# Linear attention with a SoLU feed-forward: 24 early steps change engine, and the later steps get a new order

## The chip, the cores and the metric

The kernel runs on one core of a Trainium2 chip. The metric is device time in microseconds for one execution. The core has one queue of instructions for each engine: TensorE (PE; its weight loads are shown apart, as PEld), VectorE (DVE), ScalarE (ACT), GpSimd (POOL), and SyncE (SP), which here only issues DMAs.

## The reference

```python
def _attn_ref(q, k, v):                     # each [8, 8, 576, 64]
    q_s = np.exp(q - np.max(q, axis=-1, keepdims=True))
    q_s = q_s / (np.sum(q_s, axis=-1, keepdims=True) + 1e-09)
    k_s = np.exp(k - np.max(k, axis=2, keepdims=True))
    k_s = k_s / (np.sum(k_s, axis=2, keepdims=True) + 1e-09)
    kv = np.einsum('bhsd,bhse->bhde', k_s, v)
    return np.einsum('bhsd,bhde->bhse', q_s, kv)
...
def _moe_ref(x, w_in, w_out, g_ln):         # x [4608, 512]
    h = x @ w_in                            # [4608, 1024]
    e = np.exp(h - np.max(h, axis=-1, keepdims=True))
    solu = h * (e / (np.sum(e, axis=-1, keepdims=True) + 1e-09))
    mu = np.mean(solu, axis=-1, keepdims=True)
    var = np.mean((solu - mu) ** 2, axis=-1, keepdims=True)
    return ((solu - mu) / np.sqrt(var + 1e-06) * g_ln) @ w_out
```

The attention's output, with the heads side by side, is x.

## The kernel before

**The work.** There are eight batches, and 36 tiles of 128 rows. For each batch the keys (steps `K0` to `K7`) and the queries (`Q0a`, `Q0b`, `Q0c`, ..., and `R` for the rests) get their softmax, the keys are multiplied with the values, and attention (`x`) gives the transposed rows of x. For each tile or pair of tiles the hidden product (`h` for one tile, `H` for a pair by seven half products instead of eight) is followed by the row work: softmax, normalization, division into a high and a low f16 part (`h`, or `U` for a pair), and the product with `w_out` (`o`, or `O` and `E` for a pair). `w`, `y`, `W`, `Z` scale and split the weights, `T` and `TO` make the sums and differences of weight blocks that the pairs need; `LQ`, `LK`, `V` are loads, `P` is warm-up work for TensorE.

**Who sets the order.** The work is written as Python generators. A string, `ORDER`, is read from left to right; each word names a generator, which goes on to its next `yield`, and this is one step. `*n` repeats the word. The string has 1819 steps. The instructions of all engines are issued in that order, so each engine's queue has its own part of it, and an instruction at the head of a queue waits for its operands while all behind it on that engine wait too.

**Who does a step.** Where the code says `on(default)`, the operation is done by the default engine, or by VectorE when the word ends in `.v`. The default of the element operations between two tensors, and of the small per-row scalars, is GpSimd; the default of casts and copies is ScalarE. The names that the diff touches are: `am`, `pi`, `p`, `ph` (lines 829 to 838: scalars of one column that the pass at line 842 needs), `z`, `var`, `r`, `rr` (scalars of the normalization), `u` (lines 172 and 174 for the high part, 852 for the low part), `split` (the same for x), `qT`, `vm` and `swap` (copies), `iw` (line 326, a difference of weight blocks), and `ob` and `ott` of `TO` (lines 1009, 1013, 1019).

**Buffers.** A second table, `SLOTS`, says for each tile in the order of its making which buffer it takes: 25 pages of SBUF, four PSUM banks, and two PSUM places `h` of 128x1024 for hidden rows. A tile that takes a used buffer waits until the former one has been read.

**The place that the prediction comes to most.** `H27` is one of the pairs in the later part. Its first steps in the code are:

```python
t2 = ps.tile([P, DF], F32, name=f"h{name_of(row_tiles[1])}", **place("h", 2))
product(t2[:, left], "11", "11")
yield
t1 = ps.tile([P, DF], F32, name=f"h{name}", **place("h", 2))
product(t1[:, left], "12", "21")
yield
cast(on(nc.scalar), w_, t2[:, left])
yield
product(t2[:, left], "s2", "t2", True)
```

So a pair's second product of the left half waits for a copy (`vw<-h`) of the first, and both wait until the two places `h` are free.

Of the kernel before, what the change touches and what calls it, by code (L numbers as in the profile page):

```python
# [17 lines left out]
P = 128  # L18
# [17 lines left out]
    ),  # L36
    "bank": (
# [3 lines left out]
    ),  # L41
    "h": (
        "0 1 0 1 0 1 0 1 0 1 0 1 0 1 0 0 1 1 0 1 1 0 0 1 1 0 0 1 1 0 0 1 1 0 0 1 "
    ),
}
ORDER = (
# [53 lines left out]
)  # L100


@with_exitstack
def linear_attention_solu_ffn(ctx: ExitStack, tc: tile.TileContext, q, k, v, w_in, w_out, g_ln, out):

# [1139 lines left out]
```

## Time and profile before

| what | value |
|---|---|
| median of three runs | 442.11 us (441.96 to 442.28) |
| the profiled execution's own time | 440.85 us |
| span of its instructions | 439.1 us |
| instructions | 9202 |
| busy share PE, DVE, ACT, POOL | 95%, 88%, 74%, 72% |
| mean granted clock of TensorE | 0.997 |

The span runs from the first to the last instruction that the profiler recorded; 1.75 us of the execution's time lie around it. The profiled execution is 1.26 us shorter than the median of the three runs, so sums are made against 440.85 us and their difference is then set against 442.11 us.

### The profile page before, as it was taken

The numbers are of one execution on the slowest core, as the hardware profiler recorded it, in microseconds if no ns is written. First come the engines' busy times: TensorE is split into PE (matmuls) and PEld (weight loads), VectorE is DVE, ScalarE is ACT, GpSimd is POOL, SyncE is SP. The second block draws the span as 40 slices with busy tenths as digits, with TensorE's granted clock in tenths as the row PEclk, the third lists the DMA queues.
The fourth block names the chain that finished last, engine by engine and source line by source line (L and its number), as shares of the span: only waits on it lengthen the run. The fifth ranks groups of instructions, "written<-read, shape, count | busy, mean of one in ns | idle before, by whom it ended". The sixth has DMA issues, their size and how long they took to land.

```text
span 439.1 us, 9202 instructions
## 1 busy us (share of the span) xinstructions
PE 417.4 (95%) x3441; PEld 218.1 (50%) x3441; DVE 385.5 (88%) x765; ACT 323.4 (74%) x555; POOL 316.1 (72%) x336
## 2 busy tenths in 40 slices
PE   2798899999999999999999999999999999999995
PEld 1444344454454444544544445445444445666885
DVE  5999999999898998889988869999999998988952
ACT  3799998696796689878875677768685686785920
POOL 4206983889998879859966888886939897778340
PEclk9999999999999999999999999999999999999998
DMA  8989788489799696499996568994533665379982
GB/s 277 409 306 315 154 152 233 91 206 245 173 223 184 150 192 135 90 224 217 186 251 146 126 147 188 247 215 95 78 72 82 111 144 104 63 172 188 231 204 73
DMA packets 182620, 77.93 MB, mean 177 GB/s; under 512 B 162088, under 2 KB 171312, under 8 KB 182576
## 3 DMA queue, kind: packets, MB, share of 16 engines
q1 hardware_dynamic: 182576, 77.35, 77.0%
q8 instruction: 27, 0.44, 0.4%
q14 instruction: 17, 0.14, 0.1%
HBM read 36.70 MB, written 9.44 MB: 105 GB/s over the span
## 4 chain that ended last, share of the span: by engine, by line
PE 73%; POOL 8%; ACT 8%; DVE 6%; issue 3%; DMA 1%; ACTq 0%; POOLq 0%; DVEq 0%
PE o L1113 24%; PE h L734 18%; PE h L811 12%; PE kv L471 3%; PE x L666 3%; PE o_2y L1049 2%; PE o_0y L1049 2%; PE o_0x L1049 1%; PE o_2z L1049 1%; PE o_0z L1049 1%; PE o_2x L1049 1%; POOL qm L523 1%; POOL r L882 1%; POOL qhl L548 1%; POOL am L829 1%
## 5 line engine op out<-in xcount | busy, mean ns | idle before, releaser
L1113 PE MATMUL o<-wo,uT 128*128 128x512 f16 x624 | 141.4, 379 | 0.0
L1113 PEld LDWEIGHTS <-uT 128*128 128x128 f16 x624 | 60.3, 98 | 72.7 <-issue 1.6
L811 PE MATMUL h<-wi,xT 128*128 128x512 f16 x240 | 54.4, 379 | 0.0
L734 PE MATMUL h<-wt,split 128*128 128x512 f16 x198 | 46.2, 379 | 0.9 <-ACT vw L172 0.9
L734 PEld LDWEIGHTS <-split 128*128 128x128 f16 x264 | 25.5, 98 | 31.7 <-issue 2.5
L457 POOL TENSOR_TENSOR km<-km,kb 128x1152 f32<-128x1152 f32 x12 | 33.6, 2808 | 4.9 <-ACT kb L435 3.2
L811 PEld LDWEIGHTS <-xT 128*128 128x128 f16 x240 | 23.1, 98 | 27.5 <-issue 0.6
L548 POOL TENSOR_TENSOR qhl<-qm,qhl 128x512 f16<-128x512 f32 x24 | 28.8, 1220 | 3.0 <-ACT qhl L172 2.9
L734 PE MATMUL h<-wi,xT 128*128 128x512 f16 x132 | 30.8, 379 | 0.1
L734 PEld LDWEIGHTS <-xT 128*128 128x128 f16 x198 | 19.1, 98 | 23.6 <-issue 1.8
L803 PE MATMUL h<-iw,xT 128*128 128x512 f32 x64 | 29.5, 602 | 1.2 <-ACT e L866 1.2
L541 POOL TENSOR_TENSOR qm<-qm,qrec 128x1024 f32<-128x1024 f32 x13 | 25.6, 1966 | 6.3 <-DVE qrec L532 6.0
L523 POOL TENSOR_TENSOR qm<-qm,qnmx 128x1024 f32<-128x1024 f32 (+1 forms) x14 | 25.3, 1810 | 5.7 <-DVE qnmx L521 5.5
L825 ACT ACTIVATE e<-h,nm,hs 128x1024 f32<-128x1024 f32 x20 | 24.0, 1202 | 0.5
L852 POOL TENSOR_TENSOR u<-e,u 128x1024 f16<-128x1024 f32 x8 | 17.6, 2200 | 9.0 <-ACT u L172 4.6
L1126 ACT ACTIVATE os<-o,rr 128x512 f32<-128x512 f32 x23 | 15.7, 684 | 11.0 <-PE o L1113 7.9
L521 DVE TENSOR_REDUCE qnmx<-qm 128x16 f32<-128x1024 f32 (+1 forms) x17 | 19.2, 1147 | 4.3 <-DMA qm<-in_q_dram 4.3
L829 POOL TENSOR_SCALAR am<-top 128x1 f32<-128x1 f32 x21 | 10.9, 518 | 15.2 <-DVE top L819 14.2
L525 ACT ACTIVATE qm<-qm 128x1024 f32<-128x1024 f32 (+1 forms) x17 | 17.1, 1003 | 5.9 <-POOL qm L523 5.9
L471 PE MATMUL kv<-vm,km 64*64 64x65 f32 x1152 | 19.3, 219 | 2.0 <-ACT km L459 0.9
L459 ACT ACTIVATE km<-km 128x1152 f32<-128x1152 f32 x16 | 18.5, 1163 | 3.4 <-POOL km L457 3.2
L471 PEld LDWEIGHTS kv<-vm,km 64*64 64x64 f32 x1152 | 18.0, 134 | 5.8 <-issue 3.3
(330 smaller groups left out, 1057.6 us busy)
## 6 DMA issues: line engine op xcount, KB each, us to landing
out_dram<-os SPq DMA_DIRECT2D x32, 256.0 KB, 3.0
km<-in_k_dram SPq DMA_DIRECT2D x7, 1152.0 KB, 7.3
vm<-in_v_dram SPq DMA_DIRECT2D x28, 288.0 KB, 4.3
qm<-in_q_dram SPq DMA_DIRECT2D x7, 1024.0 KB, 6.7
wo<-in_moe_w_in_dram SPq DMA_DIRECT2D x4, 512.0 KB, 8.8
w_in<-in_moe_w_in_dram SPq DMA_DIRECT2D x4, 512.0 KB, 9.2
wo<-in_moe_w_out_dram SPq DMA_DIRECT2D x4, 512.0 KB, 4.4
w_out<-in_moe_w_out_dram SPq DMA_DIRECT2D x4, 512.0 KB, 6.8
```

The source lines that it names most:

```text
L457: on(nc.gpsimd).tensor_tensor(km[:, ns], km[:, ns], wide, op=ALU.subtract)
L471: nc.tensor.matmul(o, km[half, n, c], vm[half, n, c], start=(m == 0 and c == 0), stop=(m == 1 and c == KC - 1))
L521: nc.vector.tensor_reduce(shaped(nmx), x, axis=AX.X, op=ALU.max, negate=True)
L523: on(nc.gpsimd).tensor_tensor(x, x, wide(nmx), op=ALU.add)
L541: on(nc.gpsimd).tensor_tensor(x, x, wide(rec), op=ALU.mult)
L548: on(nc.gpsimd).tensor_tensor(lo, y, hi, op=ALU.subtract)
L734: nc.tensor.matmul(out, lefts[left](s, i), right_block(right, r, i), start=(n == 0 and not onto), stop=(n + 1 == len(terms)), skip_group_c ...
L803: nc.tensor.matmul(h[:, ns], xT[:, kc], iw[kc][:, ns], start=(i == 0), stop=(i == NP - 1))
L811: nc.tensor.matmul(h[:, ns], xT[:, t, kc], wi[:, s, kc, ns], start=(i == 0), stop=(i == len(terms) - 1))
L825: nc.scalar.activation(e, h, AF.Exp, bias=nm, scale=hs, accum_out=z)
L1049: nc.tensor.matmul(accs[acc], t[:, j, first + f], out_block(right, s, f), start=(f == n == 0 and not onto), stop=(f + 1 == NF // 2 and n = ...
L1113: nc.tensor.matmul(o, uT[:, j, f], wo[:, s, f, cols], start=(f == 0 and j == 0 and s == 0), stop=(f == NF - 1 and j == 1))
```

## The change

The same 1819 steps are done. The first 1168 of them (up to the step `H22#1`, the second step of pair 22, some 273 us into the span) keep their order, and 24 of them change engine. The 651 later steps come in a new order, and 113 of them change engine too. `SLOTS` differs only where the later steps make their tiles. The 24 early ones are (the number of the step in its generator counts from 0):

| step | operation | before | after |
|---|---|---|---|
| Q0b#6 | copy of qT | ACT | DVE |
| V03#1 | copy of vm | DVE | ACT |
| h1#7, h16#5, h19#3 | pi, ph, pi | POOL | DVE |
| h0#15, h4#18, h12#17 | z | POOL | DVE |
| o1#0, o8#0 | rr | POOL | DVE |
| h6#8, h8#8, h11#8, h12#8, h11#19 | am, am, am, am, var | POOL | DVE |
| T#1 | iw, 128x512 | POOL | DVE |
| K4#5 | four copies of swap | ACT | DVE |
| x13#10, h19#8 | f16 cast of split, of u | ACT | DVE |
| h15#3 | pi | POOL | DVE |
| h15#5, o15#0, h20#2, h20#3 | ph, rr, am, pi | DVE | POOL |

Among the later ones, `TO#0` to `TO#3` (the four `ob<-wo` sums of 128x1024, line 1009) go from DVE to POOL. `Q6a#6`, `K7#9`, `Q7a#1` and `x29#11` (each an element operation between two tensors) go from POOL to DVE, as do the low parts of u of tiles 22 and 25. The low part of u of tile 21 goes from DVE to POOL.

```diff
--- before.py
+++ after.py
...
     "h": (
-        "0 1 0 1 0 1 0 1 0 1 0 1 0 1 0 0 1 1 0 1 1 0 0 1 1 0 0 1 1 0 0 1 1 0 0 1 "
+        "0 1 0 1 0 1 0 1 0 1 0 1 0 1 0 0 1 1 0 1 1 0 0 1 0 1 1 0 0 1 1 0 0 1 1 0 "
     ),
...
-    "K0*3 w2 K0 P Q0b V03.v Q0a Q0c.v Q0c Q0a K0.v K0 K0.v K0*2 Q0c Q0c.v w3 w2 K0*2 w3*2 Q0a x0 K0 w0*2 x0 w1*2 "
+    "K0*3 w2 K0 P Q0b.v V03 Q0a Q0c.v Q0c Q0a K0.v K0 K0.v K0*2 Q0c Q0c.v w3 w2 K0*2 w3*2 Q0a x0 K0 w0*2 x0 w1*2 "
...
-    "Q6c o15 o16 h20 S5.v Q6a o16 h21 V70 o16*2 h21.v Q6c h21 H22*2 V71 S5 TO.v K6*3 h17 Q6c.v*2 h20 Q6c Q6a V72 "
-    "H22*2 K6*2 H22*3 h21 o17.v o17 K6 H22.v H22 h21 h20*2 Q6a*2 S5 Q6a K7 H22 K6 H22*3 h19 H22*2 h20*4 K7 LQ7*2 "
-    "o17 x24 h21.v TO.v h23*4 h21*2 h22*6 K6*3 S6 K7*4 h19 TO.v K7 Q6a o19*2 TO.v o19 Q7a h21 h21.v o19*3 K7 o17*4 "
...
-    "o22 h23 K7*2 o22*2 h25*3 S7 o22 h24 h25 Q7a TO h24 h24.v Q7a.v h24 R7 K7*2 o19 TO.v*2 H27*4 h24 S7 Q7c H27*3 "
-    "x29 o21*2 h24.v o23 H27.v H27*2 h24*2 x29*2 h25 h25.v h25*2 x29*2 H27 Q7a x29.v H27*3 o21*2 TO h25 o22 o24.v "
...
+    "h20 h21 o16 h20*3 LK7 h21*2 Q6a o16 h20 Q6a Q6c o15 o16 h20 S5.v Q6a o16 h21 V70 o16*2 h21.v Q6c h21 H22*2 TO "
+    "K6 h21 K6*2 h17 h19 V72 Q6a H22.v V71 H22*2 h21 Q6c h19 K7*5 Q6a o17*3 H22*2 Q6a Q6a.v Q6c.v K6 h20*4 H22 Q6a "
...
+    "h22 h23*3 h23.v h23*2 o19 S5 o19*2 o20*2 x24.v o17 K7 K7.v K7 TO h22*2 TO R5 S6.v Q7c x27*4 o20 h22 x27 H24 "
+    "Q7a Q7a.v h23 H24 LQ7 H24 TO x27*3 TO o20*2 H24*3 h21*2 h21.v H24 TO Q6c x29*3 H24.v h21.v LQ7 H24 x27 R7 H24 "
...
+    "h25*2 o22.v o22 H27 h23 H27.v x29*2 Q7a S5 h24.v h24 H27*3 h25 h25.v o22*2 h24 h24.v H27*3 Q7a*3 K7*3 Q7c "
+    "h25*3 S7 R7 o22 h25 h24 R7*2 H27*2 x29.v TO Q7a h25 H27*2 o21 H27*2 U27.v R7.v U27 o22.v h24 o24.v o24 U27*2 "
...
```

## Rows read from the trace of the kernel before

**Rows 1.** The page: its head, and the busy time of each engine.

```profile
span 439.1 us, 9202 instructions
...
PE 417.4 (95%) x3441; PEld 218.1 (50%) x3441; DVE 385.5 (88%) x765; ACT 323.4 (74%) x555; POOL 316.1 (72%) x336
```

**Rows 2.** Busy time by windows; columns: window, length, each engine, clock, DMA share, GB/s.

```profile
0.00:21.60 21.60, 10.59 (x169) 6.10 (x169) 15.83 (x36) 11.52 (x16) 7.72 (x12) 1.00 0.94 342
21.60:62.40 40.80, 37.00 (x298) 17.89 (x299) 39.46 (x70) 39.34 (x67) 24.34 (x22) 1.00 0.89 241
62.40:173.40 111.00, 110.35 (x866) 52.07 (x866) 102.00 (x181) 87.03 (x160) 90.60 (x111) 1.00 0.82 181
173.40:275.50 102.10, 101.87 (x944) 49.46 (x944) 88.67 (x203) 77.37 (x135) 81.60 (x89) 1.00 0.80 178
...
295.00:318.80 23.80, 23.80 (x268) 11.87 (x267) 21.59 (x50) 17.82 (x31) 19.68 (x20) 1.00 0.46 85
318.80:342.00 23.20, 21.77 (x101) 9.61 (x99) 22.25 (x42) 16.45 (x26) 13.55 (x12) 1.00 0.41 88
...
434.60:439.10 4.50, 0.00 (x0) 0.00 (x0) 0.48 (x1) 0.00 (x0) 0.00 (x0) 0.71 0.51 117
```

**Rows 3.** What TensorE waited for over the whole span: total, times, longest.

```profile
PE h L734 <- ACT vw L172: 1.1, 2, 0.9
...
PE h L734 <- DVE top L770: 0.5, 1, 0.5
PE wide_out L191 <- DVE p_kv L201: 0.4, 1, 0.4
```

**Rows 4.** The chain that ended last, 280 to 335 us: start, length, what.

```profile
311.77 3.29 POOL ob L1013
...
318.85 1.30 DVE e L842 x2
...
322.26 0.49 ACT vw L172
...
330.52 0.61 DVE h L770
```

**Rows 5.** Groups of equal instructions, engine by engine: busy time, mean ns of one.

```profile
L1013 POOL TENSOR_TENSOR ob<-ob,ob 128x1024 f32<-128x1024 f32 x2 | 5.7, 2844 | 0.0
L829 POOL TENSOR_SCALAR am<-top 128x1 f32<-128x1 f32 x21 | 10.9, 518 | 15.2 <-DVE top L819 14.2 <-DVE part L411 0.8
...
L852 DVE TENSOR_TENSOR u<-e,u 128x1024 f16<-128x1024 f32 x4 | 4.9, 1233 | 0.0
L1009 DVE TENSOR_TENSOR ob<-wo 128x1024 f32<-128x1024 f16 x4 | 4.9, 1221 | 0.0
...
L172 ACT COPY qT<-qt 128x512 f32<-128x512 f32 x4 | 2.3, 576 | 0.0
L172 ACT COPY vm<-wi 128x576 f32<-128x576 f32 x3 | 1.9, 672 | 2.5 <-DMA wi<-in_v_dram 2.5
```

**Rows 6.** The timeline of DVE and of POOL, 47 to 63 us.

```profile
50.81 1.22 DVE L284 TENSOR_SCALAR gw<-gw 128x1024 int32<-128x1024 int32 x1
53.09 0.68 DVE L284 TENSOR_SCALAR gw<-gw 128x1024 int32<-128x1024 int32 x1
57.16 1.21 DVE L286 SCALAR_TENSOR_TENSOR gw<-w_out,gw 128x1024 int32<-128x1024 int32 x1
...
48.71 0.79 POOL L870 TENSOR_SCALAR z<-z,p 128x1 f32<-128x1 f32 x1
49.58 1.90 POOL L541 TENSOR_TENSOR qm<-qm,qrec 128x1024 f32<-128x1024 f32 x1
...
56.20 2.26 POOL L829 TENSOR_SCALAR am<-top 128x1 f32<-128x1 f32 x1
```

**Rows 7.** The timeline of ACT and of DVE, 166 to 179 us.

```profile
167.76 1.04 ACT L172 CAST split<-sums 128x1024 f16<-128x1024 f32 x1
...
171.24 1.34 DVE L335 SCALAR_TENSOR_TENSOR wt<-iw,s_in,wt 128x1024 f16<-128x1024 f32 x1 [1.61 <-ACT wt L333]
```

100 rows, old and new, of tables (ORDER, SLOTS) are left out of this document.

## Prediction

> **What bounds the kernel.** I began with the page's head and the busy shares [rows 1]: TensorE is busy for 417.4 of 439.1 us. The question is therefore where the other 21.7 us are, and whether the change can reach them. VectorE with 88% is the next to be full.
>
> The windows answer the first half [rows 2]. TensorE is idle for 21.60 - 10.59 = 11.01 us in the first window, for 40.80 - 37.00 = 3.80 in the second, for 111.00 - 110.35 = 0.65 in the third and 102.10 - 101.87 = 0.23 in the fourth. From 318.8 to 342.0 it is idle for 23.20 - 21.77 = 1.43, and in the last window for all 4.50 (the last pass and the store). That makes 21.62, so all the rest holds 0.1 us. The granted clock is 1.00 in every window with matmuls in it; TensorE's own work costs the same in both orders, as no matmul is added or taken away. What can be won by a new order behind 273 us is thus about those 1.43 us, since the last 4.50 us come after the last matmul and their steps keep their form.
>
> Then I looked for what ended these waits. The list of TensorE's waits [rows 3] names a copy on ScalarE (`vw`, longest 0.9) and a VectorE pass (line 770, 0.5). The chain [rows 4] shows how they came to be: GpSimd makes an `ob` difference that takes 3.29 us at 311.77, only then come its one-column scalars, and VectorE's two passes over `e` wait for these until 318.85. The read of the hidden rows by the first of those frees the place that pair 27 needs; its `vw` copy ends at 322.75 and TensorE goes on. The second wait ends when VectorE's line 770 has run at 330.52. In 318.8 to 342.0 VectorE is busy for 22.25 of 23.20 us [rows 2], so it comes late to everything there. In the window before it GpSimd was busy for 19.68 of 23.80 us.
>
> **The 24 early steps.** TensorE loses 0.65 + 0.23 us between 62.4 and 275.5 us [rows 2], so an edit there can win at most this, and loses only if a step comes late by more than its lead.
>
> First, the two copies in the first 20 us. `qT` leaves ScalarE and `vm` comes to it: 0.672 - 0.576 = 0.10 us more at worst [rows 5], ahead of the exponentials that the keys wait for. If the old place of the copy was off the path it is nothing. I take 0.04.
>
> Second, 47 to 63 us, where VectorE has hardly a gap (39.46 of 40.80 us busy in the window [rows 2]) and where the weights' scales are late: TensorE waits 0.4 us for `wide_out` [rows 3]. `pi` and `z` come to VectorE there. The trace has no row for these two on VectorE at this place. From below, an `am` or `z` that delays nothing costs nothing; from above, one takes no longer than the 0.518 us mean of the `am` group on GpSimd [rows 5], so 2 x 0.52 = 1.04. On the other side, GpSimd's `z` of 0.79 us at 48.71 is gone, and its pass over `qm` (1.90 us at 49.58) ends earlier. A VectorE pass that began under that pass took 1.22 us, and its like at 53.09 took 0.68 [rows 6]: up to 0.54 us may come back. I take +0.10, between -0.5 and +0.5, because the passes of VectorE follow each other without a gap while the end of the chain also hangs on other engines' sums.
>
> This is one place for the Trainium skill. The row shows a VectorE pass of 1.22 us beside a GpSimd pass and 0.68 us alone [rows 6], and a one-column `am` on GpSimd at 56.20 that took 2.26 us and ended at 58.46, just behind VectorE's two-tensor pass that ended at 58.37. The Trainium skill, "SBUF — State Buffer", "Who interferes with whom", says that the two engines share a pair of SBUF ports as an exclusive lock, which a VectorE instruction with two SBUF inputs also takes against a GpSimd instruction that reads SBUF, and that the loser is blocked until the other ends. The trace agrees at these two places; by that rule alone, moving work between these two engines frees nothing, and the gain of the later part would be 0 and the sum 442.11 + 0.08 = 442.2.
>
> Third, the cast of `split` at 167.76, 1.04 us, leaves ScalarE; its later work there comes earlier, and VectorE's idle 1.61 us before 171.24 [rows 7] holds the cast's time on VectorE (below: nothing; above: the 1.23 us of the nearest pass of this shape [rows 5]). Two short waits of TensorE at 173 and 179 us are for such copies and make up the 0.23 us of that window [rows 2]. I take -0.06, between -0.23 and 0.
>
> The other early edits are one-column scalars, a 128x512 difference, four swap copies and one cast of `u`. I cost them at nothing: they are hidden by TensorE's work, which between 62.4 and 275.5 us stands still for only 0.88 us, though VectorE has 111.00 - 102.00 = 9.0 and 102.10 - 88.67 = 13.4 us of idle time [rows 2] to take them. Without this cover the sum of their VectorE time, below 4 us, would be the price.
>
> **The later part.** I priced each of the 113 engine changes by the mean of the same operation on the engine that gets it. VectorE's sum falls by about 7 us, of which 4 x 1.221 = 4.9 are the `ob<-wo` sums [rows 5]; ScalarE gets some 7 more; GpSimd loses 4 net, although it takes those four sums. Then I went along the new string queue by queue, with TensorE going on without a stop from the point where the common part ends, and noted by how much each product's operands come before it. Through pair 27, VectorE in the old order is about level with TensorE (this is the place of the two waits), and in the new one up to 5 us ahead. So I let both old waits go: -1.43.
>
> New ones have to be set against this. In the new order the second product of pair 27 stands about 43 us behind the start of the new part, and the row pass of tile 25 that frees its place ends there at 41.6 to 43.1. Two later operands have leads of 0.15 and 0.25 us. Everything else leads by 0.4 us or more. For the two small leads I take 0.15 each, +0.30; from below nothing, from above both with the size of the old ones, 0.9 + 0.5 [rows 3].
>
> The price I don't know is that of `ob<-wo` on GpSimd, which before has only on VectorE. The bounds: 1.22 us (VectorE's, from below) and 3.29 us (the other `ob` difference on GpSimd, of the same shape, at its longest [rows 4]). I used 2.2, nearest to GpSimd's passes of 1.90 us [rows 6] and to the mean of 2.84 us for `ob<-ob` [rows 5]. The four are spread over the first 20 us, ahead of the scalars of tiles 22 to 25 in GpSimd's queue. At the upper bound they add 4 x (3.29 - 2.2) = 4.4 us there, of which GpSimd's idle time in the stretch takes some, and tile 25's pass comes 1 to 2.5 us late. The moved DMA issues (loads of values and queries, transposes of `u`) go along with their steps; the DMA share is 0.46 and 0.41 in the two windows about pair 27 [rows 2], so I cost them at nothing. A transpose issued behind a store on SP's queue is the way in which this could fail.
>
> **The sum**, against the profiled 440.85 us: -1.43 + 0.30 + 0.04 + 0.10 - 0.06 = -1.05, so 439.8. The profiled execution lies 1.26 us below the median of the runs, which gives 442.11 - 1.05 = 441.06, or 441.1 us. What a measurement of this kernel can tell from no change is about 0.2%, that is 0.88 us: faster is below 441.23, slower above 442.99.
>
> **The rivals.**
> *The waits only move.* VectorE takes the passes that GpSimd loses, GpSimd takes the sums, and waits of the old size come back at other pairs. For it: a pass on one engine lengthens one on the other [rows 6], and behind 342 us the old order has almost none to lose. Against it: VectorE's sum falls. The time is 442.11 - 1.43 + 1.43 + 0.08, within 0.5 of it: 441.7 to 442.7. The Trainium skill, "SBUF — State Buffer", "Who interferes with whom", by its lock speaks for this case.
> *GpSimd comes late (the slower side).* The four sums cost 3.29 us or more each; the scalars of tiles 22 to 25 queue behind them, tile 25's pass ends past the 43 us point, and pair 27 can't take its place. It decides once that pass ends more than 1.9 us behind the point (1.05 + 0.88). With passes of 3.29 us and another for each of the next two tiles, 2.5 + 0.5 us replace the gain: 442.11 - 1.05 + 3.0 = 444.1, from 443.0 to 445. For it: GpSimd's load of 19.68 of 23.80 us. Against it: the sums come early, where the queue had been emptied.
> *The early steps decide.* VectorE's chain for the scales comes 0.5 us later at 62 us and the later part gains nothing: 442.11 + 0.5 = 442.6, which falls within the first rival's band, and I count it there.
>
> **Chances.** My forecast 0.50, with its own range of 440.5 to 441.8 (0.36 of it below 441.23); the waits move 0.28 (nearly all within 0.2%); GpSimd late 0.22 (nearly all above 442.99). So faster 0.36, same 0.42, slower 0.22. The range of 440.5 to 443.4 leaves out the best of the forecast's own case and the larger half of the late case.
>
> **What would show it.** Right: TensorE's idle time from 318 to 342 us below 0.5 instead of 1.43, nothing above 0.3 elsewhere behind 275 us, `ob<-wo` on GpSimd at 2 to 2.5 us, and the end of `wide_out` within 0.3 us of where it was. Wrong: a wait of TensorE for `vw` or `ph` above 0.5 us at pairs 22 to 29, `ob<-wo` above 3 us, or a wait past 342 us, where my leads are the least sure.

## The result, and the profile after

The change makes the kernel slower: 445.72 us median (445.46 to 446.35, six runs) against 442.03 us (440.98 to 442.64, six runs) of the kernel before; the ratio is 1.0088, with a 95% interval of 1.0074 to 1.0102. The forecast was 441.1 us, with a range of 440.5 to 443.4. The profiled execution of the changed kernel took 445.77 us. The one of the kernel before took 440.85, 1.2 us less than its median, so the traces differ by more (4.9 us) than the medians do (3.7).

The page of the kernel after begins like [rows 1]:

```profile
span 444.0 us, 9189 instructions
...
PE 418.0 (94%) x3441; PEld 218.0 (49%) x3441; DVE 384.7 (87%) x783; ACT 327.8 (74%) x557; POOL 303.2 (68%) x316
```

TensorE's work is nearly as long as it was (417.4 us before). VectorE and GpSimd are busy for less time than before, and still the span is 4.9 us longer. The windows of the kernel after, cut like [rows 2], show where TensorE stands still:

```profile
62.40:173.40 111.00, 110.98 (x870) 52.43 (x869) 105.08 (x195) 86.22 (x157) 85.04 (x103) 1.00 0.82 178
173.40:275.50 102.10, 101.50 (x943) 49.20 (x941) 87.49 (x203) 76.12 (x132) 82.88 (x90) 1.00 0.81 180
275.50:295.00 19.50, 17.83 (x83) 7.99 (x83) 15.85 (x30) 13.40 (x27) 13.25 (x16) 1.00 0.89 210
295.00:318.80 23.80, 22.86 (x262) 11.15 (x261) 22.93 (x50) 19.60 (x33) 19.60 (x15) 1.00 0.53 103
318.80:342.00 23.20, 21.93 (x114) 9.78 (x112) 21.45 (x43) 18.86 (x33) 17.27 (x18) 1.00 0.54 107
342.00:434.60 92.60, 90.58 (x671) 59.40 (x670) 75.02 (x158) 62.08 (x97) 53.47 (x47) 1.00 0.69 137
```

From 62.4 to 275.5 us it is idle for 0.02 + 0.60 instead of 0.65 + 0.23 us. Then it loses 1.67, 0.94, 1.27 and 2.02 us, 5.90 in all, where the kernel before lost 1.43 and next to nothing. The list of TensorE's waits, as in [rows 3], names the same two producers, more often and longer, and two that are new:

```profile
PE h L735 <- DVE top L771: 2.5, 2, 1.7
PE h L735 <- ACT vw L173: 2.4, 3, 1.3
...
PE x L667 <- DVE sums L716: 0.8, 1, 0.8
...
PE wide_out L192 <- DVE p_kv L202: 0.3, 1, 0.3
...
PE h L735 <- DVE e L940: 0.3, 1, 0.3
```

(Line numbers are one higher here, as the string has a line more.) In order of time the waits are pair 22 at 286 us (1.67), the rows of x at 306 (0.84), pair 27 at 329 (1.27), pair 29 at 350 (0.79), pair 31 at 367 (0.93) and pair 33 at 379 (0.28).

What makes VectorE late is seen in the timeline of the kernel after; first some of its passes, then the GpSimd passes beside them:

```profile
276.62 1.98 DVE L447 TENSOR_TENSOR khalf<-km 128x1024 f32<-128x1024 f32 x1 [1.24 <-DMA km<-in_k_dram]
279.82 2.30 DVE L452 TENSOR_TENSOR ktop<-ktop,km 128x256 f32<-128x256 f32 x1
303.70 2.52 DVE L524 TENSOR_TENSOR qm<-qm,qnmx 128x1024 f32<-128x1024 f32 x1
325.20 2.90 DVE L853 TENSOR_TENSOR u<-e,u 128x1024 f16<-128x1024 f32 x1
...
275.62 1.90 POOL L542 TENSOR_TENSOR qm<-qm,qrec 128x1024 f32<-128x1024 f32 x1
279.72 2.13 POOL L853 TENSOR_TENSOR u<-e,u 128x1024 f16<-128x1024 f32 x1 [1.07 <-ACT u L173]
302.78 2.36 POOL L1014 TENSOR_TENSOR ob<-ob,ob 128x1024 f32<-128x1024 f32 x1
325.11 1.90 POOL L542 TENSOR_TENSOR qm<-qm,qrec 128x1024 f32<-128x1024 f32 x1 [0.47 <-DVE qrec L533]
```

Each VectorE pass here has two inputs in SBUF, and each begins while a GpSimd pass is running. The GpSimd passes end at 277.52, 281.85, 305.14 and 327.01; VectorE's end at 278.60, 282.12, 306.22 and 328.10. That is 1.08, 0.27, 1.08 and 1.09 us later: about the pass's own length (1.2 us for 128x1024, 0.42 for 128x256) less a short start. So the pass did not run slowly. It stood until GpSimd's pass had ended, and then ran at its usual speed. Against 1.23, 0.42, 1.22 and 1.23 us alone, these four lose 0.75 + 1.88 + 1.30 + 1.67 = 5.6 us, and all of it is counted as busy time.

The first row also shows a plain wait: the new order puts the maximum over the keys of batch 7 (`K7#0`) further ahead in VectorE's queue, before passes of pair 22. The load of these keys kept its place, and they land 1.24 us after VectorE is free for them.

### The profile page after: what moved, and what is told of

Same layout as the page of the kernel before. It is cut to its first block, busy times and chain, and to the rows that moved or that the text cites. A ratio compares the mean times of both kernels' runs of the same rounds, so it can differ in the third digit from the quotient of the medians.

```text
span 444.0 us, 9189 instructions
## 1 busy us (share of the span) xinstructions
PE 418.0 (94%) x3441; PEld 218.0 (49%) x3441; DVE 384.7 (87%) x783; ACT 327.8 (74%) x557; POOL 303.2 (68%) x316
## 4 chain that ended last, share of the span: by engine, by line
PE 60%; POOL 11%; DVE 10%; ACT 6%; DMA 6%; issue 4%; SPq 0%; POOLq 0%; ACTq 0%; DVEq 0%
PE o L1114 20%; PE h L735 12%; PE h L812 12%; PE kv L472 3%; PE x L667 2%; DMA w_out<-in_moe_w_out_dram 2%; PE o_2y L1050 2%; DMA km<-in_k_dram 2%; POOL ob L1014 2%; PE o_0y L1050 1%; POOL ob L1010 1%; DMA uT_0c<-u_0c 1%; PE o_2z L1050 1%; PE o_2x L1050 1%; ACT qm L526 1%
## 5 line engine op out<-in xcount | busy, mean ns | idle before, releaser
L458 POOL TENSOR_TENSOR km<-km,kb 128x1152 f32<-128x1152 f32 x11 | 31.4, 2865 | 4.7 <-DMA wo<-in_moe_w_out_dram 3.2
L542 POOL TENSOR_TENSOR qm<-qm,qrec 128x1024 f32<-128x1024 f32 x14 | 28.1, 2009 | 7.0 <-DVE qrec L533 6.4
L549 POOL TENSOR_TENSOR qhl<-qm,qhl 128x512 f16<-128x512 f32 x22 | 25.6, 1182 | 9.2 <-ACT qhl L173 9.2
L524 POOL TENSOR_TENSOR qm<-qm,qnmx 128x1024 f32<-128x1024 f32 (+1 forms) x13 | 23.8, 1832 | 5.6 <-DVE qnmx L522 5.6
L836 POOL TENSOR_TENSOR p<-pi,mone 128x1 f32<-128x1 f32 x26 | 16.5, 633 | 5.5 <-DVE pi L833 4.3
L529 DVE TENSOR_REDUCE qsum<-qm 128x16 f32<-128x1024 f32 (+1 forms) x17 | 19.5, 1145 | 0.3 <-ACT qm L526 0.2
```

What stands on the lines that cost most here:

```text
L458: on(nc.gpsimd).tensor_tensor(km[:, ns], km[:, ns], wide, op=ALU.subtract)
L524: on(nc.gpsimd).tensor_tensor(x, x, wide(nmx), op=ALU.add)
L542: on(nc.gpsimd).tensor_tensor(x, x, wide(rec), op=ALU.mult)
L549: on(nc.gpsimd).tensor_tensor(lo, y, hi, op=ALU.subtract)
```

## The experiments

The theories in the expectations: L, the loss begins at the late load of keys and goes on along VectorE's queue; E, the early engine changes make part of it; S, the four sums on GpSimd make it; P, passes of VectorE and GpSimd hold each other up, and which one comes first decides; C, they only share memory and slow down a little; D, VectorE simply has too much to do. Ratios are to the kernel before, which was measured beside each kernel on the same chip (its median there was 442.2 to 443.0 us).

**The two parts apart.** `early_only` has the old order and buffers with the 24 early engine changes; `late_only` has the new order with the old engines up to step 1168.

```diff
 early_only, against the kernel before (two of the 24)
-h19 V73 h20.v h21 o16 h20.v h20*2 LK7
+h19 V73 h20 h21 o16 h20*3 LK7
...
 late_only, against the changed kernel
-h19 V73 h20 h21 o16 h20*3 LK7
+h19 V73 h20.v h21 o16 h20.v h20*2 LK7
```

> The order and the buffers of the kernel before, with the engines of its first 1168 steps as in the changed kernel: the 24 early engine changes alone. Theory L (the loss begins where VectorE waits for the keys of batch 7 and goes on along VectorE's queue, all of it in the later part): TensorE's idle time from 62.4 to 275.5 us went from 0.88 to 0.63 us between the two traces, so this kernel should come out 0 to 0.4 us below the one before, 441.6 to 442.0. Theory E (the early engine changes make part of the loss): 1 us or more above it, 443 or more.

> The changed kernel with the old engines in its first 1168 steps: the new later order alone. Theory L: the whole loss stays, 3.5 to 4.2 us above the kernel before, 445.5 to 446.2, and the wait of pair 22 for VectorE's line 771 stays at 1.5 to 2 us. Theory E: 1 us or more below the changed kernel, 444.7 or less.

The early changes alone cost 0.31% (ratio 1.0031, 1.0016 to 1.0046; 444.24 us), the later part alone 0.53% (1.0053, 1.0035 to 1.0071; 445.59 us). Theory L was wrong on the first and E right: TensorE's waits up to 275 us do get shorter, but two new ones follow in pair 22, of 1.65 and 0.67 us, in an order that hasn't changed there, and a third of 0.87 at 406 us. The timeline of the kernel before:

```profile
273.68 0.75 DVE L174 CAST qhl<-qm 128x512 f16<-128x512 f32 x2
...
274.92 2.69 POOL L852 TENSOR_TENSOR u<-e,u 128x1024 f16<-128x1024 f32 x1 [2.08 <-ACT u L172]
```

And of `early_only`:

```profile
274.57 2.69 DVE L175 CAST qhl<-qm 128x512 f16<-128x512 f32 x2
...
274.59 2.38 POOL L853 TENSOR_TENSOR u<-e,u 128x1024 f16<-128x1024 f32 x1 [0.85 <-ACT u L173]
```

In the kernel before the same two casts took 0.75 us and were through before GpSimd began. Now VectorE comes 0.9 us later, the second cast meets GpSimd's pass, and ends 0.29 us behind its end (276.97).

The result of `late_only` is not so clear. The ratios add up to about the 0.88%, as E has it. But the median of `late_only` is L's (445.59 against 445.72 for the changed kernel, which was measured beside other executions of the kernel before), and so is pair 22's wait, 1.78 us. Behind 275.5 us TensorE loses 6.08 us there, as much as in the changed kernel (5.90). What the early changes cost in the new order therefore stays open. Pair 22's wait is made up in another way in `late_only`:

```profile
277.69 1.23 DVE L447 TENSOR_TENSOR khalf<-km 128x1024 f32<-128x1024 f32 x1 [2.69 <-DMA km<-in_k_dram]
...
279.68 2.38 DVE L451 TENSOR_TENSOR ktop<-khalf 128x256 f32<-128x256 f32 x1
...
279.65 2.13 POOL L853 TENSOR_TENSOR u<-e,u 128x1024 f16<-128x1024 f32 x1 [2.88 <-ACT u L173]
```

VectorE waits longer for the keys there, 2.69 us, and only one pass is held up (2.38 instead of 0.43).

**The lock measured by itself.**

```diff
     with tc.manual_schedule():
         in_turns(ORDER)
+        side_by_side()
...
+        for beside in (False, True):
+            for work in passes:
+                nc.scalar.copy(src, one_in)
+                if beside:
+                    nc.gpsimd.tensor_tensor(g_out, src, g_in, op=ALU.subtract)
+                nc.vector.tensor_scalar(col, src[:, 0:1], 2.0, 1.0, op0=ALU.mult, op1=ALU.mult)
+                nc.vector.tensor_scalar(col, col, 2.0, 1.0, op0=ALU.mult, op1=ALU.mult)
+                work()
```

> The kernel before with a measuring piece behind its last step: six kinds of VectorE passes, each once alone and once started just after a GpSimd difference of 128x1024 on other tiles, and twice a one-column GpSimd step beside a VectorE difference. Its own time says nothing. Theory P (a VectorE pass with two inputs in SBUF, or a copy or scaling from SBUF to SBUF, waits until GpSimd's running pass has ended, and the other way round): the difference, the cast and the 16-column scaling end 0 to 1.1 us after the end of GpSimd's pass, at about 2 us longer than alone; the pass over PSUM, the copy from PSUM and the maximum keep their lengths within 0.1 us; the one-column step ends behind VectorE's difference. Theory C (both engines only slow each other as far as they share memory): all lengthen by a similar share, none by more than half.

The timeline of `side_by_side`, one execution: five of the six passes of VectorE alone, then beside GpSimd (with one of the one-column scalings between them), then three of GpSimd's passes, and one-column steps of GpSimd, one beside a VectorE pass and one alone. The sixth, the copy from PSUM, took 1.21 us both times.

```profile
441.14 1.22 DVE L1234 TENSOR_TENSOR bench<-bench,bench 128x1024 f32<-128x1024 f32 x1
443.78 1.27 DVE L1235 SCALAR_TENSOR_TENSOR bench<-hbench,bcol,bench 128x1024 f32<-128x1024 f32 x1
446.48 1.21 DVE L1236 TENSOR_REDUCE bcol<-bench 128x1 f32<-128x1024 f32 x1
449.11 0.68 DVE L1237 CAST bench<-bench 128x1024 f16<-128x1024 f32 x1
452.60 0.17 DVE L1239 TENSOR_SCALAR bden<-bsum 128x16 f32<-128x16 f32 x1
453.79 0.15 DVE L1247 TENSOR_SCALAR bz<-bz 128x1 f32<-128x1 f32 x1
453.86 3.20 DVE L1234 TENSOR_TENSOR bench<-bench,bench 128x1024 f32<-128x1024 f32 x1
458.49 1.27 DVE L1235 SCALAR_TENSOR_TENSOR bench<-hbench,bcol,bench 128x1024 f32<-128x1024 f32 x1
461.99 1.21 DVE L1236 TENSOR_REDUCE bcol<-bench 128x1 f32<-128x1024 f32 x1
465.48 2.67 DVE L1237 CAST bench<-bench 128x1024 f16<-128x1024 f32 x1
473.08 2.15 DVE L1239 TENSOR_SCALAR bden<-bsum 128x16 f32<-128x16 f32 x1
476.31 1.23 DVE L1251 TENSOR_TENSOR bench<-bench,bench 128x1024 f32<-128x1024 f32 x1 [1.08 <-ACT bench L1250]
...
453.65 2.34 POOL L1245 TENSOR_TENSOR bench<-bench,bench 128x1024 f32<-128x1024 f32 x1 [29.99 <-ACT bench L1243]
465.27 2.34 POOL L1245 TENSOR_TENSOR bench<-bench,bench 128x1024 f32<-128x1024 f32 x1 [1.16 <-ACT bench L1243]
472.86 2.34 POOL L1245 TENSOR_TENSOR bench<-bench,bench 128x1024 f32<-128x1024 f32 x1 [1.15 <-ACT bench L1243]
476.39 1.33 POOL L1253 TENSOR_SCALAR bam<-bench 128x1 f32<-128x1 f32 x1 [1.19 <-ACT bench L1250]
477.82 0.29 POOL L1255 TENSOR_SCALAR bpi<-bam 128x1 f32<-128x1 f32 x1
```

Three kinds of VectorE pass wait for the end of GpSimd's pass: the difference of two SBUF tiles (1.22 to 3.20; it ends at 457.06, GpSimd at 455.99), the cast from SBUF to SBUF (0.68 to 2.67) and the scaling of only 16 columns (0.17 to 2.15). The pass with one input in PSUM and the maximum keep their 1.27 and 1.21 us, and a scaling of one column takes 0.15 us while GpSimd's pass runs (453.79). In the other direction a one-column step of GpSimd takes 1.33 instead of 0.29 us and ends 0.18 us after VectorE's difference. This is theory P; C is out. From here on "the lock" means this: the one pass stands until the other has ended.

**The early part: is it the lock, or the 0.9 us?** Both kernels start from `early_only`.

```diff
 cast_act
-V71 S5 TO.v K6*3 h17 Q6c.v*2 h20 Q6c Q6a V72
+V71 S5 TO.v K6*3 h17 Q6c Q6c.v h20 Q6c Q6a V72
...
 h20_back
-h19 V73 h20 h21 o16 h20*3 LK7
+h19 V73 h20.v h21 o16 h20.v h20*2 LK7
```

> The kernel with the 24 early engine changes alone, with one more change: the f16 casts of the queries of batch 6 (step Q6c#5, 0.75 us on VectorE in the kernel before, 2.69 us here) go to ScalarE. Theory P: the two waits of pair 22 (1.65 and 0.67 us) go, as there is no cast left that GpSimd's pass holds up; 0.9 to 2.3 us below the kernel with the early changes alone, within 0.8 us of the kernel before. Theory D (VectorE comes 0.9 us late out of the early steps and is just too busy): VectorE is relieved of 0.75 us, the waits fall from 2.3 to about 1.5 us.

> The kernel with the 24 early engine changes alone, with two of them undone: am and pi of tile 20 stay on VectorE. VectorE then doesn't wait 1.1 us for GpSimd's ph at 266 us. Theory P: its cast of the queries comes some 0.6 us earlier, at 273.9 instead of 274.57, ahead of GpSimd's pass at 274.59, and the waits of pair 22 fall from 2.3 to 0.5 us or less: within 0.6 us of the kernel before. Theory D: the waits fall by the 0.6 us that VectorE comes earlier, to about 1.7.

`cast_act`: 442.36 us, ratio 1.0004 (0.9992 to 1.0016). Both waits of pair 22 are gone, though VectorE still comes 0.9 us late; one of 0.62 us is new, at the fourth step of pair 22. Theory P is right on the size, D not. The edit moves GpSimd too: its pass begins at 275.80 instead of 274.59, as ScalarE hands it its input later, so the differences behind the casts come ahead of it as well. `h20_back`: ratio 1.0026 (1.0011 to 1.0041), with waits of 0.86 and 0.67. Here P's number was wrong, and D's (waits of about 1.7 us) was the nearer one. The timeline shows how:

```profile
273.58 0.75 DVE L175 CAST qhl<-qm 128x512 f16<-128x512 f32 x2
...
274.25 3.22 DVE L549 TENSOR_TENSOR qhl<-qm,qhl 128x512 f16<-128x512 f32 x2
...
274.39 2.53 POOL L853 TENSOR_TENSOR u<-e,u 128x1024 f16<-128x1024 f32 x1 [1.64 <-ACT u L173]
```

The casts are through in 0.75 us, as expected. But GpSimd's pass begins 0.2 us earlier as well, and the next two differences, 1.29 us in the kernel before, meet it and take 3.22. An engine that comes earlier doesn't win the race by that; who is first at each pass does.

**The later part: the load, the sums, one pass.** All start from the changed kernel.

```diff
 load_first
-h19.v K6 h19 Q6c h21 h19 o18 h19 V73 h20 h21 o16 h20*3 LK7 h21*2
+h19.v K6 h19 LK7 Q6c h21 h19 o18 h19 V73 h20 h21 o16 h20*3 h21*2
...
 sums_back
-H22*2 TO K6 ... K7.v K7 TO h22*2 TO R5 ... LQ7 H24 TO x27*3
+H22*2 TO.v K6 ... K7.v K7 TO.v h22*2 TO.v R5 ... LQ7 H24 TO.v x27*3
...
 sums_out
-                on(nc.gpsimd).tensor_tensor(x, wo[:, 0, rows, cols], wo[:, 1, rows, cols], op=ALU.add)
+                nc.scalar.copy(x, wo[:, 0, rows, cols])
...
 copy_behind
-Q7a S5 h24.v h24 H27*3
+Q7a h24.v h24 S5 H27*3
```

> The changed kernel with one DMA issue moved: the load of the keys of batch 7 goes ahead of one store and one load on SP's queue, some 2.2 us earlier. Nothing else moves. Theory L: VectorE's idle 1.24 us ahead of the first key maximum goes, and with it the 0.75 and 1.88 us by which two passes are longer beside GpSimd, if they no longer meet GpSimd's passes; pair 22's wait of 1.67 falls to 0 to 0.5 and the time to 444.1 to 444.6. Theory S (the four sums on GpSimd hold up the scalars of the later tiles, and these set the time): the next waits take over what is won, within 0.4 us of the changed kernel, 445.3 to 446.1.

> The changed kernel with the four sums of output weight blocks (TO#0 to TO#3) on VectorE again, at their new places in the order. Theory S: GpSimd loses 8.5 us of passes of 2.12 us each ahead of the scalars of tiles 22 to 25, the waits at 306 and 328 us (0.84 and 1.27) go in the main: 443.7 to 444.7. Theory L: VectorE is the one that is late there, and gets 4 x 1.22 = 4.9 us more; slower than the changed kernel by 1 to 3 us, 446.7 to 448.7.

> The changed kernel with the four sums TO#0 to TO#3 left out of GpSimd: each block is a copy of the high part of the weights alone, made on ScalarE (the low part is left out of these blocks, so part of the output differs from the reference). GpSimd has 4 x 2.13 = 8.5 us less to do between 272 and 303 us, and ScalarE some 4 us more. Theory P (the passes of the two engines hold each other up): VectorE's two small steps and its pass over qm between 295 and 306 us (0.55, 0.99 and 2.52 us) fall by 1 to 2.5 us in all, the wait at 306 us (0.84) goes, the wait of pair 22 at 286 us (1.67) stays: 0.5 to 1.5 us below the changed kernel. Theory S (the sums alone make the loss): 2.5 us or more below it.

> The changed kernel with one copy of 0.17 us (step S5#2, on VectorE) moved behind the step that follows it, the low part of u of tile 24. Theory P: that pass then starts at 325.00, ahead of GpSimd's pass over qm at 325.11, and takes 1.2 us instead of 2.90; the wait of pair 27 (1.27 us) falls below 0.2, and the time by 0.8 to 1.3 us, unless a later pass meets GpSimd anew. Theory D (VectorE has too much to do there): the same work in another order of two neighbours; the wait stays at 1.1 to 1.3 us and the time within 0.3 us of the changed kernel.

`load_first` came out at 449.08 us, ratio 1.0147 (1.0124 to 1.0171): 0.6% slower than the changed kernel, which neither theory had. From its timeline:

```profile
275.66 1.21 DVE L448 TENSOR_TENSOR khalf<-km 128x1024 f32<-128x1024 f32 x1
276.90 2.27 DVE L450 TENSOR_TENSOR khalf<-khalf 128x512 f32<-128x512 f32 x1
...
276.55 0.69 ACT L1128 ACTIVATE os<-o,rr 128x512 f32<-128x512 f32 x1 [4.75 <-DMA out_dram<-os]
```

The first maximum neither waits nor is held up, as expected, though the load goes out only 1.0 us earlier, and not 2.2; the next one meets GpSimd in its place (2.27 us instead of 0.69). What makes the kernel slower, by the chain of waits, is another thing: the load of 1152 KB now stands ahead of a store on SP's queue, the store's buffer comes free late, and ScalarE stands for 4.75 us. Its cast of u then begins at 282.05 instead of 278.60, GpSimd's pass follows late, and four differences of VectorE meet that pass (4.43 us instead of 2.49). Pair 22 waits 2.22 and 2.38 us. What the load's wait alone costs stays open.

`sums_back`: 448.47 us, ratio 1.0126 (1.0105 to 1.0146), slower than the changed kernel as theory L had it: the wait for the rows of x grew from 0.84 to 2.17 us, pair 27's stayed at 1.27, and pair 22's moved from its last product (1.67) to its fourth step (1.34). The sums are better off on GpSimd than on VectorE in this order. `sums_out`, with a copy on ScalarE in place of each sum, which leaves the low part out: 444.16 us, ratio 1.0048 (1.0029 to 1.0066). That is 1.6 us below the changed kernel, just past P's 1.5 and short of S's 2.5; where it came from is not as P had it. Pair 22's wait, which was to stay, fell from 1.67 to 0.23:

```profile
276.75 1.23 DVE L447 TENSOR_TENSOR khalf<-km 128x1024 f32<-128x1024 f32 x1 [1.40 <-DMA km<-in_k_dram]
...
279.20 0.42 DVE L452 TENSOR_TENSOR ktop<-ktop,km 128x256 f32<-128x256 f32 x1
...
274.95 1.90 POOL L542 TENSOR_TENSOR qm<-qm,qrec 128x1024 f32<-128x1024 f32 x1 [1.39 <-DVE qrec L533]
...
280.12 2.13 POOL L853 TENSOR_TENSOR u<-e,u 128x1024 f16<-128x1024 f32 x1 [2.09 <-ACT u L173]
```

Here VectorE waits longer for the load than in the changed kernel, 1.40 us, and does the same work. But GpSimd has no sum to make, so its pass over `qm` begins 0.67 us earlier and ends at 276.85, 0.1 us behind the start of the first of these two; the second is through before GpSimd's next pass. They take 1.23 and 0.42 instead of 1.98 and 2.30 us. So most of pair 22's wait in the changed kernel is the lock, not the load. The wait at 306 us is gone too, with the pass over `qm` at 1.22 us instead of 2.52; the copies put on ScalarE bring one of 1.64 us for a `vw` copy in pair 24.

`copy_behind`: 445.40 us, ratio 1.0069 (1.0045 to 1.0093), 0.3 us by its median below the changed kernel, 0.8 by the ratios. P had 0.8 to 1.3, D up to 0.3, so the time alone doesn't tell them apart; the waits do.

```profile
325.08 1.16 DVE L854 TENSOR_TENSOR u<-e,u 128x1024 f16<-128x1024 f32 x1
326.27 1.75 DVE L630 COPY hsr<-hs 64x2 f32<-64x2 f32 x1
...
325.31 2.69 POOL L543 TENSOR_TENSOR qm<-qm,qrec 128x1024 f32<-128x1024 f32 x1 [0.47 <-DVE qrec L534]
```

Two neighbours in VectorE's queue exchanged, and the pass takes 1.16 instead of 2.90 us; now GpSimd is the one that waits (2.69 for 1.90), and pair 27's wait of 1.27 is gone. But the copy of two columns that was put behind takes 1.75 instead of 0.17 us, and the last product of pair 27 waits 1.03 us. The lock decides; who pays is in the main only moved.

**Order and engines apart.** The new order and buffers, with every engine as before:

```diff
-H22*2 TO K6 h21 K6*2 h17 h19 V72 Q6a H22.v V71
+H22*2 TO.v K6 h21 K6*2 h17 h19 V72 Q6a H22 V71
```

> The new order and buffers with all engines as in the kernel before (neither the 24 early nor the 113 later engine changes). If order and engines could be priced apart, as the prediction did, the order alone would cost within 3 us of the kernel before. Theory P (which pass meets which decides): the old engines put VectorE's and GpSimd's passes beside each other in places that neither kernel has; more than 5 us slower.

A single execution: 489.90 us, some 47 us above the kernel before. The later order is good only with its own engines. Their prices can't be added up apart, as the prediction did. How much of it is the lock this execution doesn't show: TensorE's own busy time is 12 us longer (429.7 against 417.4), with a mean granted clock of 0.91 to 0.96 in five of its six windows behind 275.5 us (342 to 488 us taken in three), below full speed for a part of each, against 1.00 in the kernel before; the rest are waits.

**A version that beats both.** Pair 27 of the kernel before is helped by ScalarE, whose cast of 128x1024 keeps its 1.04 us beside a GpSimd pass (in `pair27` at 330.23, GpSimd from 330.40 on); then the nine early engine changes ahead of step 638 are added.

```diff
 pair27, against the kernel before
-h24.v Q7a.v h24 R7 K7*2 o19 TO.v*2 H27*4 h24 ... x29*2 h25 h25.v h25*2 x29*2 H27
+h24.v Q7a.v h24 H27*3 R7 K7*2 o19 TO.v H27 h24 ... x29*2 h25*2 TO h25*2 x29*2 H27
...
 pair27_early: and the table's changes from Q0b#6 to h8#8, among them
-K0*3 w2 K0 P Q0b V03.v Q0a
+K0*3 w2 K0 P Q0b.v V03 Q0a
```

> The kernel before with pair 27 helped in another way: its first copy (H27#2, ScalarE) goes ahead of an exponential of 0.62 us and a copy of 0.40 us on ScalarE, and the f16 cast of u of tile 25 and one of the cast weight blocks (TO#8) go from VectorE to ScalarE, which is idle for 2.98 us there and is never held up by GpSimd. Theory P: both waits of pair 27 (0.91 and 0.52) go, and no VectorE pass is put beside a GpSimd pass anew: 0.8 to 1.4 us below the kernel before. Theory D (what VectorE does less comes back as a wait of another pair): within 0.4 us of it.

> The kernel of the run before this one, and in addition those of the 24 early engine changes that lie ahead of step 638 (before 160 us): they took TensorE's wait of 0.58 us at 132.5 us away. Theory P: 0.3 to 0.6 us below the run without them, as long as the shift moves no VectorE pass behind a GpSimd pass later; if it does, up to 2 us above it. Theory D: 0.3 to 0.6 below.

`pair27`: 441.65 us, ratio 0.9989 (0.9970 to 1.0007), not clear of no change, so it bears out neither P nor D. In its trace the first wait of pair 27 is gone and 0.25 us of the second is left, but TensorE lost 2.04 us from 62.4 to 275.5, where the steps are those of the kernel before and its trace lost 0.88: executions differ by as much as there is to win. `pair27_early`: 440.29 us against 442.40, ratio 0.9950 (0.9935 to 0.9965), faster than both kernels; it is 1.4 us below `pair27`, more than the 0.3 to 0.6 expected, and why is not shown. Its windows about pair 27 show what is left of 1.43 us, 0.25:

```profile
295.00:318.80 23.80, 23.80 (x267) 11.80 (x266) 22.02 (x50) 17.45 (x30) 19.79 (x19) 1.00 0.49 88
318.80:342.00 23.20, 22.95 (x107) 10.24 (x105) 21.85 (x42) 19.72 (x31) 14.69 (x14) 1.00 0.42 90
```

## Why the prediction was wrong

**The step that failed** is the price of an engine change, "by the mean of the same operation on the engine that gets it", with VectorE's sum "about 7 us" lower and, from that, +0.30 us for new waits. The new waits behind 275.5 us came to 5.90 us. VectorE's busy time fell by 3.8 us with the later part alone (381.7 in `late_only` against 385.5). On VectorE the low part of u took 1.55 us in the mean of five after the change against 1.23 of four before [rows 5], and a pass over `qm` 2.52 us against 1.22 in `sums_out`. A mean holds for the neighbours that its passes happened to have. The prediction had the evidence in hand, a scaling of 1.22 instead of 0.68 us and an `am` that ended just behind VectorE's pass [rows 6], read it as a rival that would bring the gain to 0, and gave that 0.28. It didn't see that the same rule can make the kernel slower, and that lowering an engine's busy sum is no gain if the passes are put beside each other. The Trainium skill, "SBUF — State Buffer", "Who interferes with whom", had it right, in kind and for either engine as the one that waits. `side_by_side` agrees with it for all the passes it tried.

**The early steps** "at nothing" failed in the old order, where they cost 0.31%; in the new order their share stays open (`late_only`). Their idle cover was there, and TensorE gained between 62 and 275 us. The cost came behind them: `am` and `pi` of tile 20 on GpSimd made VectorE wait 1.09 us for `ph` at 266 us, and the shift put a cast beside a GpSimd pass. That such a shift can matter past its own stage wasn't in the sum; `cast_act` and `h20_back` show that it's the meeting and not the shift that costs.

**"Everything else leads by 0.4 us or more"** failed at pair 22, at the very start of the new part: the passes were laid end to end with their lengths alone. The load of the keys, which isn't among the "moved DMA issues" that were costed at nothing, since its reader moved and not it, lands 1.24 us late for that reader's new place.

**What was right.** `ob<-wo` on GpSimd takes 2.13 us (2.2 was taken); the upper bound of 3.29 us was itself a pass held up (VectorE's difference for `split` ran until 312.85 us, over a microsecond behind its start), the same difference takes 2.37 in the mean of four now. `wide_out` waits 0.35 instead of 0.40 us. The two old waits of pair 27 did go, and a third, of 1.27 us, took their place. GpSimd was not the one that came late: tile 25's pass cost TensorE nothing at pair 27's second product, so the slower rival, with 444.1 the nearest of the three times though its band ends at 445, came near for a wrong reason. Two rows were misread, without weight in the sum: 330.52 is the start of VectorE's line 770 and not its end, and the `x2` at 318.85 is one pass over `e` with the read of its sum.

**Still open.** What the early changes cost in the new order, as said. The waits at 350, 367 and 379 us (2.0 us) were not tried one by one. That the lock makes them too is argued from the lengths of passes beside them (a scaling of 16 columns took 1.24 us at 345.88), not shown.

## What to carry to other kernels

Before moving work between VectorE and GpSimd, sort VectorE's passes by whether they have two inputs in SBUF, or copy, cast or scale more than one column from SBUF to SBUF: these are the ones that stood still here while a GpSimd pass ran, and their shortest length, not their mean, is what they cost with no GpSimd pass beside them. Where such a pass is late for TensorE, move it to ScalarE, or change which of the two comes first, and look again at the next pass, since the wait moves on. A changed order and its changed engines are one thing, and are priced together by who stands beside whom.

## What the runs showed that was not expected

A VectorE copy of two columns took 1.75 us and a scaling of 16 columns 2.15, so small steps can pay as much as large ones. A load of 1152 KB put ahead of a store on the same queue held ScalarE up for 4.75 us through the store's buffer. And single executions of the kernel before ranged from 440.3 to 444.5 us, while the prediction took 0.2%, 0.88 us, for what can be told from no change.
